# Rows of eight tokens cast by the DMA, masks made by GpSimd, and a new order of sums and scalings in the head of an attention and feed-forward kernel

## The chip, the cores and the metric

The kernel runs on one core of one Trainium2 chip. The metric is the device time of the program in microseconds (us). Each kernel was run beside the kernel before, on the same chip, several rounds in turn. A ratio is the mean time of a kernel's fast runs over that of the kernel before beside it, so it is not quite the ratio of the medians that are quoted. The experiments are compared with each other and with the change by medians, although they did not all run together; the kernel before was at 361.9 to 362.2 us in every group. All runs in this study were in the fast state.

## The reference, cut to what matters

```python
# q, k, v: (8 batches, 8 heads, 576 tokens, 64), f32
rel = pos[:, None] - pos[None, :]
mask_plain = (rel >= 0) & (rel < 32)                            # heads 0 to 3
mask_dil   = (rel >= 0) & (rel < 128) & (rel % 4 == 0)          # heads 4 to 7
attn = softmax(where(mask, q @ k.T / 8, -1e9)) @ v
x = attn.transpose(0, 2, 1, 3).reshape(4608, 512)
out = ((gelu(x @ w_gate) * (x @ w_val)) @ w_out)                # 512 -> 1536 -> 512
```

## The kernel before

One unit of attention is two heads of one batch. The kernel runs the four units of batch 0 alone (the head), then starts the feed-forward on 512 tokens at a time and hides the other units beside it. Dilated heads are split by token modulo 4, so q and k must be transposed with four tokens to a row. These are the loads and helpers that the change touches:

```python
def quads(src, b, h0, lo, hi):           # four tokens to a row: 128 rows + a rest of 16 rows
    return src[b, h0 : h0 + HK, lo:hi, :].rearrange("h (p r) d -> p h (r d)", r=4)

def load_qk_dil(b):                      # GpSimd's queue, cast f32 -> f16 by the DMA
    qd = ldp.tile([P, 2, HK, 4, D], F16, ...); rd = ldp.tile([16, 2, HK, 4, D], F16, ...)
    for t, src in ((0, q), (1, k)):
        nc.gpsimd.dma_start(out=fl(qd[:, t]), in_=quads(src, b, HK, 0, 4 * P))
    for t, src in ((0, q), (1, k)):
        nc.gpsimd.dma_start(out=fl(rd[:, t]), in_=quads(src, b, HK, 4 * P, S))
```

The head itself, in program order (cut):

```python
# plain q, k of batch 0 on the SP and ACT queues (f32); identity and masks from DRAM on GpSimd's
for t, src, eng in ((0, q, nc.sync), (1, k, nc.scalar)):
    eng.dma_start(out=fh(first_d[t]), in_=quads(src, 0, HK, 0, 4 * P))     # dilated, f32
    eng.dma_start(out=fh(first_r[t]), in_=quads(src, 0, HK, 4 * P, S))
v_plain(0, sv0, nc.sync)                                                   # values, f32
...
load_v_dil_rest(0)
load_w(0)                        # first block of gate and value weights
v_cast(0, sv0)                   # GpSimd; waits for the values
copy("pool", tiles["v", 0][1], r4(first_vd))
w1 = load_w(1)
load_w(2)
...
emit_s(0, 4, pe_mask=True); emit_s(1, 0, pe_mask=True)      # scores of units 0 and 1
...                                                         # den(): sums, num(): numerators
num(2, 0); num(3, 2)
gate["dma"] = w1
...                              # batch 1: plain q, k on SP's queue, then
qd1, rd1 = load_qk_dil(1)
load_wo(0)
... cast_six("pool", q61, st1, t, hp)                       # needs batch 1's plain q and k
wo1 = load_wo(1); wo2 = load_wo(2)
```

In the first feed-forward pass (c == 0) TensorE transposes batch 1 between column blocks: dilated after blocks 8 and 11, plain after blocks 9 and 10. The prediction calls each of these places a hook.

The softmax here doesn't subtract the row's maximum and nothing guards it: scores larger than these inputs give would overflow.

Of the kernel before, what the change touches and what calls it, by code (L numbers as in the profile page):

```python
# [9 lines left out]
F16 = mybir.dt.float16  # L10
F32 = mybir.dt.float32
# [7 lines left out]


def _np_masks():
    p = np.arange(128)[:, None]

    def band(n, off=0):
        rel = np.arange(n)[None, :] + off - p
        return (rel >= 0) & (rel < WIN)

    main_p, last_p, tail_p = band(160), band(128), band(64, 64)
    main_d = band(128)

    rel = 48 + np.arange(16)[None, :] - p % 64
    rest_d = [(rel >= 0) & (rel < WIN) & (p // 64 == m) for m in range(2)]
    mp = np.concatenate([main_p, main_p, main_p, last_p, tail_p], axis=1).astype(np.float16)
    md = np.concatenate([main_d, rest_d[0], main_d, rest_d[1]], axis=1).astype(np.float16)
    return mp, md
# [3 lines left out]
def kernel(  # L39
# [19 lines left out]
    R6 = S // 6  # L59
    NCH = NT // CH  # L60
# [10 lines left out]

    mp_np, md_np = _np_masks()
    mp_dram = nc.inline_tensor(mp_np, name="mask_plain")
    md_dram = nc.inline_tensor(md_np, name="mask_dil")
    id_dram = nc.inline_tensor(np.eye(P, dtype=np.float16), name="attn_identity")
    id32_dram = nc.inline_tensor(np.eye(16, dtype=np.float32), name="identity_f32")
# [13 lines left out]
    ident32 = const.tile([16, 16], F32, tag="ident32")  # L90
# [31 lines left out]
    first_d = [x32[t][:, 0 : HK * 4 * D] for t in range(2)]  # L122
    first_r = [x32[2 + t][0:16, 0 : HK * 4 * D] for t in range(2)]
# [21 lines left out]
    def quads(src, b, h0, lo, hi):  # L145

        return src[b, h0 : h0 + HK, lo:hi, :].rearrange("h (p r) d -> p h (r d)", r=4)
# [4 lines left out]
    def fh(t):  # L152
        return t.rearrange("p (h c) -> p h c", h=HK)

    def sixes(src, b):

        return src[b, 0:HK, :, :].rearrange("h (p r) d -> p h (r d)", r=6)

# [44 lines left out]
    def load_qk_dil(b):  # L203
        qd = ldp.tile([P, 2, HK, 4, D], F16, tag="qd", name=f"qd{b}")
        rd = ldp.tile([16, 2, HK, 4, D], F16, tag="rd", name=f"rd{b}")
        for t, src in ((0, q), (1, k)):
            nc.gpsimd.dma_start(out=fl(qd[:, t]), in_=quads(src, b, HK, 0, 4 * P))
        for t, src in ((0, q), (1, k)):
            nc.gpsimd.dma_start(out=fl(rd[:, t]), in_=quads(src, b, HK, 4 * P, S))
        return qd, rd  # L210

# [44 lines left out]
    def copy(eng, dst, src):  # L256
        if eng == "act":
            nc.scalar.copy(dst, src)
        elif eng == "pool":
            nc.gpsimd.tensor_copy(dst, src)  # L260
        else:
            nc.vector.tensor_copy(dst, src)
# [21 lines left out]
    def t_dil(b, hp, qd, q0, k0, engs):  # L284

        qtd_ = tiles["qT", b][1]
        for t, c0 in ((0, q0), (1, k0)):
            for hl in range(2):
                for m in range(2):
                    nc.tensor.transpose(  # L290
                        ps16f[:, c0 + (2 * hl + m) * P : c0 + (2 * hl + m + 1) * P],
                        qd[:, t, 2 * hp + hl, 2 * m : 2 * m + 2, :].rearrange("p r d -> p (r d)"),
                        ident,
                    )
        for t, c0 in ((0, q0), (1, k0)):
            copy(
                engs[t],
                qtd_[:, t, 2 * hp : 2 * hp + 2].rearrange("p h m i -> p (h m) i")[:, :, 0:P],
                ps16f[:, c0 : c0 + 512].rearrange("p (c i) -> p c i", i=P),
            )  # L300

    def t_rest(b, hp, rd, r0):

        qtd_ = tiles["qT", b][1]
        f32 = rd[0].dtype == F32
        pv = (psf if f32 else ps16f)[:, r0 : r0 + P]
        for t in range(2):
            for hl in range(2):
                for m in range(2):
                    c0 = (4 * t + 2 * hl + m) * 16  # L310
                    h0 = (2 * hp + hl) * 4 * D + 2 * m * D
                    nc.tensor.transpose(
                        pv[:, c0 : c0 + 16], rd[t][:, h0 : h0 + P], ident32 if f32 else ident[0:16, 0:16]
                    )
        nc.vector.tensor_copy(
            qtd_[:, :, 2 * hp : 2 * hp + 2].rearrange("p t h m i -> p t (h m) i")[:, :, :, P:NCL],
            pv.rearrange("p (t c i) -> p t c i", t=2, i=16),
        )
# [262 lines left out]
    def warm(n, bank):  # L581
        for _ in range(n):
            nc.tensor.matmul(ps[:, bank, :], ones[:, 0:P], ones, start=True, stop=True)
# [4 lines left out]
    nc.gpsimd.dma_start(ident, id_dram.ap())  # L588
    nc.gpsimd.dma_start(mask_p, mp_dram.ap())
    for t, src, eng in ((0, q, nc.sync), (1, k, nc.scalar)):  # L590
        eng.dma_start(out=fh(first_d[t]), in_=quads(src, 0, HK, 0, 4 * P))
        eng.dma_start(out=fh(first_r[t]), in_=quads(src, 0, HK, 4 * P, S))
    nc.gpsimd.dma_start(ident32, id32_dram.ap())
    nc.gpsimd.dma_start(mask_d, md_dram.ap())
# [5 lines left out]
    qd0 = ldp.tile([P, 2, HK, 4, D], F16, tag="qd", name="qd0")  # L600
# [3 lines left out]

    def r4(t):
        return fh(t).rearrange("p h (r d) -> p h r d", r=4)

    warm(16, 7)
# [6 lines left out]
    nc.vector.tensor_scalar(bias_p, mask_p, 1.0, 60000.0, ALU.subtract, ALU.mult)  # L615
    for hp in range(2):
        t_plain(0, q6, hp, 2 * hp, ("act", "dve"))
    nc.gpsimd.tensor_scalar(bias_d, mask_d, 1.0, 60000.0, ALU.subtract, ALU.mult)
    for hp in range(2):
        copy("pool", qd0[:, 0, 2 * hp : 2 * hp + 2], r4(first_d[0])[:, 2 * hp : 2 * hp + 2])  # L620
    load_v_dil_rest(0)
    load_w(0)
    v_cast(0, sv0)
    copy("pool", tiles["v", 0][1], r4(first_vd))
    w1 = load_w(1)
    load_w(2)
# [8 lines left out]

    emit_s(0, 4, pe_mask=True)
    emit_s(1, 0, pe_mask=True)
    for hp, eng in ((0, "dve"), (1, "act")):
        copy(eng, qd0[:, 1, 2 * hp : 2 * hp + 2], r4(first_d[1])[:, 2 * hp : 2 * hp + 2])
    den(0, 4, wide=True)  # L640
    for hp in range(2):
        t_dil(0, hp, qd0, 4096 + 1024 * hp, 4608 + 1024 * hp, ("act", "dve"))
    for hp in range(2):
        t_rest(0, hp, first_r, P * hp)
    last_keys(0, 0, HK)
    den(1, 4, wide=True)
    emit_s(2, 0, pe_mask=True)
    num(0, 4)
    den(2, 4, wide=True)
    emit_s(3, 0, pe_mask=True)  # L650
    num(1, 4)
    den(3, 4, wide=True)
    num(2, 0)
    num(3, 2)
# [8 lines left out]
    qd1, rd1 = load_qk_dil(1)  # L663
# [28 lines left out]
    for c in range(NCH):  # L692
# [11 lines left out]
        for nb in range(NNB):  # L704
# [19 lines left out]
            if c == 0 and nb in (8, 11):  # L724
                rr = rd1.rearrange("p t h r d -> p t (h r d)")
                hp = nb // 11
                t_dil(1, hp, qd1, 4096 + 512 * hp, 5120 + 512 * hp, ("dve", "dve"))
                t_rest(1, hp, (rr[:, 0], rr[:, 1]), 6144 + P * hp)
# [109 lines left out]
```

## Time and profile before

| | |
|---|---|
| time before, median | 362.28 us (361.33 to 362.37, 3 runs) |
| span of the profiled run | 359.8 us, TensorE (PE) busy 344.5 us |
| first feed-forward matmul | 25.77 us |
| first column pair of the feed-forward done | 30.55 us |
| batch 1's first transpose | 42.64 us |
| first matmul of the output projection | 50.54 us |

In the page and in the timelines, each line gives an engine, a line of the kernel, an operation and what it reads and writes. A bracket at the end says how long the engine had been idle, and what ended that. The granted clock is the share of TensorE's full clock that it was given in a stretch. The prediction below shows the lines of before that carry the reading. Three more of the timeline of before matter later. They are the second place where TensorE meets a load (columns: start us, length us, engine, line, operation):

```profile
42.64 0.61 PE L290 MATMUL ps<-ident,qd 128*128 128x128 f16 x8
43.18 0.38 PE L312 MATMUL ps<-ident,rd 16*128 16x16 f16 x8
43.49 1.04 PE L533 MATMUL ps<-xT,wg 128*128 128x512 f16 x4
```

There is no bracket: batch 1's dilated q and k arrive just in time, and nothing is lost. By the view of the transfers, k's 128 rows land 18.7 us after their issue at 24.05, at 42.75, and its 16 rows 17.6 us after 25.69, at 43.29. "Just in time" is what I failed to see as a danger.

### The profile page before, as it was taken

The numbers are of one execution on the slowest core, as the hardware profiler recorded it, in microseconds if no ns is written. First come the engines' busy times: TensorE is split into PE (matmuls) and PEld (weight loads), VectorE is DVE, ScalarE is ACT, GpSimd is POOL, SyncE is SP. The second block draws the span as 40 slices with busy tenths as digits, with TensorE's granted clock in tenths as the row PEclk, the third lists the DMA queues.
The fourth block names the chain that finished last, engine by engine and source line by source line (L and its number), as shares of the span: only waits on it lengthen the run. The fifth ranks groups of instructions, "written<-read, shape, count | busy, mean of one in ns | idle before, by whom it ended". The sixth has DMA issues, their size and how long they took to land.

```text
span 359.8 us, 5997 instructions
## 1 busy us (share of the span) xinstructions
PE 344.5 (96%) x2358; PEld 166.2 (46%) x2358; DVE 196.0 (54%) x298; ACT 145.9 (41%) x212; POOL 78.2 (22%) x110
## 2 busy tenths in 40 slices
PE   6789999999989999899999999999999999999995
PEld 2554454444544445444444444544454444444442
DVE  3584446744266325765479838893679613403320
ACT  2633355244542345433653356436543123312321
POOL 2580434450531342063003410140000000000000
PEclk9959999999999999999999999999999999999999
DMA  8999999999999897599438952795100020011002
GB/s 208 232 183 215 209 159 195 199 141 239 192 119 228 178 157 144 139 168 153 94 106 186 148 97 88 178 168 68 60 29 0 21 97 2 1 66 52 0 29 87
DMA packets 107291, 45.30 MB, mean 126 GB/s; under 512 B 83040, under 2 KB 102496, under 8 KB 107264
## 3 DMA queue, kind: packets, MB, share of 16 engines
q1 hardware_dynamic: 84272, 31.21, 40.1%
q0 software_dynamic: 21456, 12.01, 25.8%
q10 hardware_dynamic: 1536, 1.70, 2.1%
q8 instruction: 18, 0.29, 0.3%
q14 instruction: 9, 0.07, 0.1%
HBM read 40.13 MB, written 9.44 MB: 138 GB/s over the span
## 4 chain that ended last, share of the span: by engine, by line
PE 88%; DVE 5%; DMA 3%; ACT 1%; issue 1%; ACTq 0%
PE ps L533 47%; PE ps L564 26%; PE ps L442 5%; PE ps L545 4%; DMA xT<-in_k_dram 3%; PE ps L369 2%; PE ps L339 1%; DVE dt L500 1%; DVE rb L507 1%; DVE xT L521 1%; PE ps L355 1%; PE ps L455 1%; PE ps L332 1%; ACT P L371 1%; DVE rc L505 0%
## 5 line engine op out<-in xcount | busy, mean ns | idle before, releaser
L558 DVE SCALAR_TENSOR_TENSOR u_all<-g,ps 128x512 f16<-128x512 f16 x108 | 72.6, 683 | 75.8 <-PE ps L533 65.7
L557 ACT ACTIVATE g<-ps 128x512 f16<-128x512 f32 x108 | 63.6, 597 | 123.6 <-PE ps L533 109.4
L564 PE MATMUL ps<-wo,u_all 128*128 128x512 f16 x432 | 100.9, 380 | 0.4 <-ACT osb L575 0.3
L533 PE MATMUL ps<-xT,wg 128*128 128x512 f16 x392 | 100.6, 379 | 0.2
L533 PE MATMUL ps<-xT,wv 128*128 128x512 f16 x392 | 100.6, 379 | 0.0
L564 PEld LDWEIGHTS <-u_all 128*128 128x128 f16 x432 | 39.2, 98 | 44.6 <-issue 0.5
L533 PEld LDWEIGHTS <-wv 128*128 128x128 f16 x392 | 38.3, 98 | 46.4 <-issue 0.2
L533 PEld LDWEIGHTS <-wg 128*128 128x128 f16 x392 | 37.3, 98 | 44.6 <-issue 2.1
L575 ACT ACTIVATE osb<-ps 128x512 f32<-128x512 f32 x33 | 19.7, 597 | 48.4 <-PE ps L564 48.4
L500 DVE STREAM_TRANSPOSE dt<-ps 128x576 f32<-128x576 f32 x25 | 19.5, 779 | 25.7 <-PE ps L442 25.6
L199 POOL CAST qp<-st 128x2048 f16<-128x2048 f32 x6 | 11.4, 1893 | 99.5 <-DMA st<-in_k_dram 61.3
L507 DVE STREAM_TRANSPOSE rb<-rc 128x576 f32<-128x576 f32 x32 | 24.9, 778 | 1.1
L371 ACT ACTIVATE P<-ps 128x1152 f16<-128x1152 f32 x16 | 18.1, 1129 | 13.1 <-PE ps L369 13.0
L349 ACT ACTIVATE P<-ps 128x960 f16<-128x960 f32 x16 | 15.5, 970 | 9.2 <-PE ps L339 9.1
L521 DVE TENSOR_TENSOR xT<-ps,rb 128x576 f16<-128x576 f32 x16 | 17.8, 1124 | 0.3
L545 PE MATMUL ps<-xT,wg 128*128 128x512 f16 x40 | 16.0, 400 | 1.4 <-DVE xT L521 0.9
L577 DVE TENSOR_SCALAR osb<-ps 128x512 f32<-128x512 f32 x3 | 2.1, 692 | 27.8 <-PE ps L564 27.8
L545 PE MATMUL ps<-xT,wv 128*128 128x512 f16 x40 | 15.9, 398 | 0.0
L442 PE MATMUL ps<-P,ones 128*64 128x192 f16 (+5 forms) x174 | 11.6, 248 | 2.0 <-ACT P L371 1.0
L379 DVE TENSOR_TENSOR P<-P,mask_p 128x1344 f16<-128x1344 f16 x10 | 9.1, 917 | 6.8 <-ACT P L350 6.8
L379 DVE TENSOR_TENSOR P<-P,mask_d 128x1152 f16<-128x1152 f16 x8 | 6.1, 757 | 11.1 <-ACT P L371 11.1
L470 DVE STREAM_TRANSPOSE dt<-ps 64x576 f32<-64x576 f32 x14 | 10.9, 781 | 0.4
(83 smaller groups left out, 268.4 us busy)
## 6 DMA issues: line engine op xcount, KB each, us to landing
out_dram<-osb SPq DMA_DIRECT2D x36, 256.0 KB, 2.0
sv<-in_v_dram SPq DMA_DIRECT2D x40, 128.0 KB, 3.5
st<-in_q_dram SPq DMA_DIRECT2D x24, 128.0 KB, 3.2
st<-in_k_dram SPq DMA_DIRECT2D x24, 128.0 KB, 2.9
qd<-in_q_dram POOLq DMA_DIRECT2D x7, 256.0 KB, 5.0
qd<-in_k_dram POOLq DMA_DIRECT2D x7, 256.0 KB, 6.7
vd<-in_v_dram POOLq DMA_DIRECT2D x7, 256.0 KB, 7.1
wg<-in_moe_w_gate_dram POOLq DMA_DIRECT2D x3, 512.0 KB, 7.7
```

The source lines that it names most:

```text
L349: nc.scalar.activation(pt[:, :, 0:PB], sb[:, 0, :, 0:PB], AF.Exp, bias=0.0, scale=scale)
L371: nc.scalar.activation(pt, ps[:, b0 : b0 + 4, 0:DW], AF.Exp, bias=0.0, scale=scale)
L442: nc.tensor.matmul(o, lhs, rhs, start=st, stop=True, skip_group_check=True)
L500: nc.vector.transpose(dst, den)
L507: nc.vector.transpose(rb.rearrange("p (b c) -> p b c", c=32), bass.AP(tensor=rc.tensor, offset=rc.offset, ap=[rc.ap[0], [1, 18], [0, 32]]),)
L521: nc.vector.tensor_tensor(dst.rearrange("p (i m s) -> p i m s", m=2, s=2), num, rb.rearrange("p (s m i) -> p i m s", s=2, m=2), ALU.mult,)
L533: nc.tensor.matmul(ps[:, b0 + gi, :], w[:, kc, ns], xT[kc][:, tok], start=(kc == 0), stop=(kc == NKC - 1))
L545: nc.tensor.matmul(ps[:, pairs[nb] + gi, :], w[:, kc, ns], xT[kc][:, tok], start=(kc == 0), stop=(kc == NKC - 1),)
L557: nc.scalar.activation(g, ps[:, b0, :], AF.Gelu)
L558: nc.vector.scalar_tensor_tensor(u_all[:, nb, :], g, USCALE, ps[:, b0 + 1, :], ALU.mult, ALU.mult)
L564: nc.tensor.matmul(ps[:, bank, :], u_all[:, fc, tb * P : (tb + 1) * P], wo_t[fc // 4][:, fc % 4, :], start=(fc == 0), stop=(fc == NNB - 1),)
L575: nc.scalar.activation(osb, ps[:, bank, :], AF.Copy, bias=0.0, scale=1.0 / USCALE)
```

## The change

Its intent: fewer bytes and casts in the head, and less for VectorE (DVE) to do there. Batches 0 and 1 load dilated q and k in 72 rows of eight tokens, cast by the DMA. Identity and masks are made by GpSimd (POOL). The sums of batch 0 get their own PSUM banks, and two units are scaled by GpSimd. Core of the diff, cuts marked:

```diff
+def load_eights(b):
+    q8 = ldp.tile([R8, 2, HK, 8, D], F16, tag="qd", name=f"qd{b}")        # R8 = 72
+    for t, src in ((0, q), (1, k)):
+        nc.gpsimd.dma_start(out=q8[:, t].rearrange("p h r d -> p h (r d)"), in_=eights(src, b, HK, H))
...
-nc.gpsimd.dma_start(ident, id_dram.ap()); nc.gpsimd.dma_start(mask_p, mp_dram.ap())   # and mask_d
-    eng.dma_start(out=fh(first_d[t]), ...); eng.dma_start(out=fh(first_r[t]), ...)
+mask_plain()                     # GpSimd: fill, six affine selects
+qd0 = load_eights(0)
+mask_dil()
...
 load_v_dil_rest(0)
-load_w(0)
 v_cast(0, sv0)
+load_w(0)
...
+def num_split(n, b0):
+    emit_pv(n, b0, ("num",))
+    rb = tiles.pop(("rb", n))
+    nc.scalar.copy(first_n[n], psf[:, b0 * 512 : b0 * 512 + S])
+    nc.gpsimd.tensor_tensor(xT[n][:, 0:S], first_n[n], rb, ALU.mult)
...
+t_dil(0, 0, qd0, 4, ("dve", "dve")); t_dil(0, 1, qd0, 6, ("act", "act"))
+... copy("pool", tiles["v", 0][1], r4(first_vd)); w1 = load_w(1)
+den(0, 0, wide=True); den(1, -2, wide=True)
+emit_s(2, 4, ...); emit_s(3, 0, ...)
+num_split(0, 4); den(2, 4, ...); num_split(1, 0); ...; den(3, 4, ...); norm_x(2, 2); num(3, 0)
+load_w(2)
...
-qd1, rd1 = load_qk_dil(1)
+qd1 = load_eights(1)
```

More of the change, by code (lines that the diff above doesn't have):

```diff
@@ L18 @@
 USCALE = 32.0
-def _np_masks():
-    p = np.arange(128)[:, None]
-    def band(n, off=0):
-        rel = np.arange(n)[None, :] + off - p
-        return (rel >= 0) & (rel < WIN)
-    main_p, last_p, tail_p = band(160), band(128), band(64, 64)
-    main_d = band(128)
-    rel = 48 + np.arange(16)[None, :] - p % 64
-    rest_d = [(rel >= 0) & (rel < WIN) & (p // 64 == m) for m in range(2)]
-    mp = np.concatenate([main_p, main_p, main_p, last_p, tail_p], axis=1).astype(np.float16)
-    md = np.concatenate([main_d, rest_d[0], main_d, rest_d[1]], axis=1).astype(np.float16)
-    return mp, md
 @with_exitstack
@@ L59 @@
     R6 = S // 6
+    R8 = S // 8
     NCH = NT // CH
@@ L70 @@
     ctx.enter_context(tc.manual_schedule())
-    mp_np, md_np = _np_masks()
-    mp_dram = nc.inline_tensor(mp_np, name="mask_plain")
-    md_dram = nc.inline_tensor(md_np, name="mask_dil")
-    id_dram = nc.inline_tensor(np.eye(P, dtype=np.float16), name="attn_identity")
-    id32_dram = nc.inline_tensor(np.eye(16, dtype=np.float32), name="identity_f32")
     const = ctx.enter_context(tc.tile_pool(name="const", bufs=1))
@@ L89 @@
     ident = const.tile([P, P], F16, tag="ident")
-    ident32 = const.tile([16, 16], F32, tag="ident32")
     mask_p = const.tile([P, PH], F16, tag="mask_p")
@@ L121, with band, mask_plain, mask_dil @@
     first_p = u32[0:R6, :].rearrange("p (t h c) -> p t h c", t=2, h=HK)
-    first_d = [x32[t][:, 0 : HK * 4 * D] for t in range(2)]
-    first_r = [x32[2 + t][0:16, 0 : HK * 4 * D] for t in range(2)]
+    first_n = [x32[g][:, 0:S] for g in range(2)]
+    nc.gpsimd.memset(ident, 1.0)
+    for sign in (1, -1):
+        nc.gpsimd.affine_select(
+            out=ident, in_=ident, pattern=[[sign, P]], compare_op=ALU.is_ge, fill=0.0, base=0, channel_multiplier=-sign
+        )
+    def band(t, step, off):
+        for sign, base in ((1, off), (-1, WIN - 1 - off)):
+            nc.gpsimd.affine_select(
+                out=t,
+                in_=t,
+                pattern=[[sign * step, t.shape[1]], [sign, t.shape[2]]],
+                compare_op=ALU.is_ge,
+                fill=0.0,
+                base=base,
+                channel_multiplier=-sign,
+            )
+    def mask_plain():
+        nc.gpsimd.memset(mask_p, 1.0)
+        band(mask_p[:, 0:PB].rearrange("p (r c) -> p r c", c=PW), 0, 0)
+        band(mask_p[:, PB : PB + P].rearrange("p (r c) -> p r c", r=1), 0, 0)
+        band(mask_p[:, PB + P : PH].rearrange("p (r c) -> p r c", r=1), 0, 64)
+        nc.vector.tensor_scalar(bias_p, mask_p, 1.0, 60000.0, ALU.subtract, ALU.mult)
+    def mask_dil():
+        nc.gpsimd.memset(mask_d, 1.0)
+        by_class = mask_d.rearrange("p (m i) -> p m i", m=2)
+        band(by_class[:, :, 0:P], 0, 0)
+        band(by_class[:, :, P:NCL], 64, 48)
     def load_w(i):
@@ L157, in sixes, with eights @@
         return src[b, 0:HK, :, :].rearrange("h (p r) d -> p h (r d)", r=6)
+    def eights(src, b, h0, h1):
+        return src[b, h0:h1, :, :].rearrange("h (p r) d -> p h (r d)", r=8)
     def rows(src, b, kb):
@@ L210, in load_qk_dil @@
         return qd, rd
+    def load_eights(b):
+        q8 = ldp.tile([R8, 2, HK, 8, D], F16, tag="qd", name=f"qd{b}")
+        for t, src in ((0, q), (1, k)):
+            nc.gpsimd.dma_start(out=q8[:, t].rearrange("p h r d -> p h (r d)"), in_=eights(src, b, HK, H))
+        return q8
     def load_v_dil(b):
@@ L282, in t_plain, with t_dil @@
             )
-    def t_dil(b, hp, qd, q0, k0, engs):
+    def t_dil(b, hp, q8, b0, engs):
         qtd_ = tiles["qT", b][1]
-        for t, c0 in ((0, q0), (1, k0)):
+        for t in range(2):
             for hl in range(2):
-                for m in range(2):
+                for r in range(4):
+                    c0 = ((hl * 2 + r % 2) * 2 + r // 2) * R8
                     nc.tensor.transpose(
-                        ps16f[:, c0 + (2 * hl + m) * P : c0 + (2 * hl + m + 1) * P],
-                        qd[:, t, 2 * hp + hl, 2 * m : 2 * m + 2, :].rearrange("p r d -> p (r d)"),
-                        ident,
+                        ps16[:, b0 + t, c0 : c0 + R8],
+                        q8[:, t, 2 * hp + hl, 2 * r : 2 * r + 2, :].rearrange("p r d -> p (r d)"),
+                        ident[0:R8, 0:R8],
                     )
-        for t, c0 in ((0, q0), (1, k0)):
             copy(
                 engs[t],
-                qtd_[:, t, 2 * hp : 2 * hp + 2].rearrange("p h m i -> p (h m) i")[:, :, 0:P],
-                ps16f[:, c0 : c0 + 512].rearrange("p (c i) -> p c i", i=P),
-            )
-    def t_rest(b, hp, rd, r0):
-        qtd_ = tiles["qT", b][1]
-        f32 = rd[0].dtype == F32
-        pv = (psf if f32 else ps16f)[:, r0 : r0 + P]
-        for t in range(2):
-            for hl in range(2):
-                for m in range(2):
-                    c0 = (4 * t + 2 * hl + m) * 16
-                    h0 = (2 * hp + hl) * 4 * D + 2 * m * D
-                    nc.tensor.transpose(
-                        pv[:, c0 : c0 + 16], rd[t][:, h0 : h0 + P], ident32 if f32 else ident[0:16, 0:16]
-                    )
-        nc.vector.tensor_copy(
-            qtd_[:, :, 2 * hp : 2 * hp + 2].rearrange("p t h m i -> p t (h m) i")[:, :, :, P:NCL],
-            pv.rearrange("p (t c i) -> p t c i", t=2, i=16),
-        )
+                qtd_[:, t, 2 * hp : 2 * hp + 2].rearrange("p h m (i u) -> p (h m) i u", u=2),
+                ps16[:, b0 + t, 0:S].rearrange("p (c u i) -> p c i u", c=4, u=2),
+            )
     def emit_s(n, b0, pe_mask=False):
@@ L587 @@
         eng.dma_start(out=first_p[:, t], in_=sixes(src, 0))
-    nc.gpsimd.dma_start(ident, id_dram.ap())
-    nc.gpsimd.dma_start(mask_p, mp_dram.ap())
-    for t, src, eng in ((0, q, nc.sync), (1, k, nc.scalar)):
-        eng.dma_start(out=fh(first_d[t]), in_=quads(src, 0, HK, 0, 4 * P))
-        eng.dma_start(out=fh(first_r[t]), in_=quads(src, 0, HK, 4 * P, S))
-    nc.gpsimd.dma_start(ident32, id32_dram.ap())
-    nc.gpsimd.dma_start(mask_d, md_dram.ap())
+    mask_plain()
+    qd0 = load_eights(0)
+    mask_dil()
     sv0 = new_v(0)
@@ L599 @@
     q6 = ldp.tile([R6, 2, 6, HK, D], F16, tag="qp", name="qp0")
-    qd0 = ldp.tile([P, 2, HK, 4, D], F16, tag="qd", name="qd0")
     new_qt(0)
-    def r4(t):
-        return fh(t).rearrange("p h (r d) -> p h r d", r=4)
-    warm(16, 7)
+    warm(22, 7)
     for vp_, _, vt_, _ in vset:
@@ L614, with r4 @@
             cast_six(("dve", "act")[t], q6, first_p, t, hp)
-    nc.vector.tensor_scalar(bias_p, mask_p, 1.0, 60000.0, ALU.subtract, ALU.mult)
     for hp in range(2):
         t_plain(0, q6, hp, 2 * hp, ("act", "dve"))
-    nc.gpsimd.tensor_scalar(bias_d, mask_d, 1.0, 60000.0, ALU.subtract, ALU.mult)
-    for hp in range(2):
-        copy("pool", qd0[:, 0, 2 * hp : 2 * hp + 2], r4(first_d[0])[:, 2 * hp : 2 * hp + 2])
+    nc.vector.tensor_scalar(bias_d, mask_d, 1.0, 60000.0, ALU.subtract, ALU.mult)
     load_v_dil_rest(0)
+    v_cast(0, sv0)
     load_w(0)
-    v_cast(0, sv0)
-    copy("pool", tiles["v", 0][1], r4(first_vd))
-    w1 = load_w(1)
-    load_w(2)
+    def r4(t):
+        return fh(t).rearrange("p h (r d) -> p h r d", r=4)
     def den(n, b0, wide=False):
@@ L634, in num @@
         norm_x(n, b0)
+    def num_split(n, b0):
[3 more added lines that the diff above has]
+        nc.gpsimd.tensor_tensor(xT[n][:, 0:S], first_n[n], rb, ALU.mult)
     emit_s(0, 4, pe_mask=True)
     emit_s(1, 0, pe_mask=True)
-    for hp, eng in ((0, "dve"), (1, "act")):
-        copy(eng, qd0[:, 1, 2 * hp : 2 * hp + 2], r4(first_d[1])[:, 2 * hp : 2 * hp + 2])
-    den(0, 4, wide=True)
-    for hp in range(2):
-        t_dil(0, hp, qd0, 4096 + 1024 * hp, 4608 + 1024 * hp, ("act", "dve"))
-    for hp in range(2):
-        t_rest(0, hp, first_r, P * hp)
-    last_keys(0, 0, HK)
-    den(1, 4, wide=True)
-    emit_s(2, 0, pe_mask=True)
-    num(0, 4)
+    t_dil(0, 0, qd0, 4, ("dve", "dve"))
+    t_dil(0, 1, qd0, 6, ("act", "act"))
+    last_keys(0, 0, 2)
+    last_keys(0, 2, HK, nc.gpsimd)
+    copy("pool", tiles["v", 0][1], r4(first_vd))
+    w1 = load_w(1)
+    den(0, 0, wide=True)
+    den(1, -2, wide=True)
+    emit_s(2, 4, pe_mask=True)
+    emit_s(3, 0, pe_mask=True)
+    num_split(0, 4)
     den(2, 4, wide=True)
-    emit_s(3, 0, pe_mask=True)
-    num(1, 4)
+    num_split(1, 0)
+    emit_pv(2, 2, ("num",))
     den(3, 4, wide=True)
-    num(2, 0)
-    num(3, 2)
+    norm_x(2, 2)
+    num(3, 0)
+    load_w(2)
     gate["dma"] = w1
@@ L724 @@
             if c == 0 and nb in (8, 11):
-                rr = rd1.rearrange("p t h r d -> p t (h r d)")
-                hp = nb // 11
-                t_dil(1, hp, qd1, 4096 + 512 * hp, 5120 + 512 * hp, ("dve", "dve"))
-                t_rest(1, hp, (rr[:, 0], rr[:, 1]), 6144 + P * hp)
+                t_dil(1, nb // 11, qd1, 6 - 2 * (nb // 11), ("dve", "dve"))
             if nb == NNB - 1 and c > 0 and s_list:
```

## The prediction

> **What bounds the kernel now.** I read first the page's slices of the span, then the chain of waits in order of time, then the timeline of the first 31 us engine by engine, the DMA issues of the first 45 us, and the table of 5 us windows.
>
> The slices tell which part of the kernel can move at all:
>
> ```profile
> PE   6789999999989999899999999999999999999995
> PEclk9959999999999999999999999999999999999999
> ```
>
> One slice is 9 us. TensorE (PE) is full from the fourth slice on; only the first three are thin, and the granted clock falls only in the third (18 to 27 us). In the table of windows PE is busy 5.00 of every 5 us from 25 to 55 us. After the head the kernel is a stream of matmuls which the change touches only where batch 1 is transposed. So the question is: when do the first feed-forward matmuls (L545) begin, and at what clock?
>
> The chain of waits (start us, length us, what) answers the first half:
>
> ```profile
> 1.19 12.33 DMA xT<-in_k_dram
> 14.07 0.78 DVE dt L500
> 15.17 0.78 DVE rb L507
> 15.95 0.64 DVE qTd L262 x2
> ...
> 24.10 1.73 PE ps L442 x24
> 25.83 4.88 PE ps L545 x16
> 30.72 12.09 PE ps L533 x56
> ```
>
> For 12.3 us the chain is one transfer, the dilated k of batch 0 in f32, landing at 13.52. Then follow 12.3 us of short steps to 25.8. The first 16 feed-forward matmuls take 4.9 us instead of some 3.45 (16 at the 0.216 us between starts that the timeline shows at full clock), because they begin at half clock: the windows give a granted clock of 0.50 in 20 to 25 us and 0.65 in 25 to 30 us.
>
> The timeline (start us, us, engine, line, operation) shows VectorE (DVE) is the busiest on that path, and GpSimd (POOL) spends its time on issuing:
>
> ```profile
> 13.54 0.60 DVE L262 CAST qd<-xT 128x512 f16<-128x512 f32 x1 [2.18 <-DMA xT<-in_k_dram]
> 19.20 0.78 DVE L507 STREAM_TRANSPOSE rb<-rc 128x576 f32<-128x576 f32 x1
> 20.04 0.76 DVE L518 TENSOR_TENSOR xT<-ps,rb 128x576 f16<-128x576 f32 x1
> 10.37 1.19 POOL L618 TENSOR_SCALAR bias_d<-mask_d 128x288 f16<-128x288 f16 x1 [6.82 <-DMA mask_d<-mask_dil]
> 16.64 0.78 POOL L128 DMA_DIRECT2D wv<-in_moe_w_val_dram  x1
> ```
>
> A second limit lies just under the first. The view of the tile wv gives 8.8 us as its shortest issue-to-landing time. Its first issue at 16.64 plus 8.8 is 25.4, and PE takes it at 25.8. So DMA must come earlier too if the start is to move.
>
> [...] masks issued on the software queue at 1.9 and 3.0 us landed 7.8 and 7.3 us later, while 1.15 MB of plain q and k was running. [...] the clock falls after the transposes of 13.9 to 17.5 us, and matmul spacing returns from 0.43 to 0.22 us at 28.3, 2.5 us after the dense stream begins.
>
> **The change part by part.**
>
> *Loads.* The masks (168, 72, 32 and 1 KB) are no longer loaded. Dilated q and k of batch 0 leave the hardware queues and are cast by the DMA. Cost: over the first 45 us, plain transfers on the SP queue use 28.4% of 45 us for 3.02 MB, 4.2 us per MB; the software queue uses 66.4% for 4.67 MB written, 6.4 us per MB. Before, 1.18 MB plain is 5.0 us and masks some 1.7 us; after, 0.59 MB cast is 3.8 us. Saving: 2.9 us of DMA time. But GpSimd issues this load only after building mask_p. Its casts run at 1.0 to 1.3 ns per column, its two-step bias at 4.1; I take 1.75 plus 0.15 us per instruction as an estimate for a select. Identity: 256 columns, two instructions, 0.75 us. Plain mask: 1344 columns, six instructions, 3.25 us. Fills: 0.8 us. Begun at 0.6, this ends at 5.4; two issues of 0.8 end at 7.0. Before, the same load was issued at 1.2. And values, formerly behind it, now compete. From 2.0 us: plain q and k 4.8 us, values (1.15 MB) 4.9, casting load 3.8, sum 13.5, so all lands by about 15.5. [...] k at T = 14.8. The same sum for before (2.0 + 4.8 + 5.0 + 1.7 = 13.5) hits the observed 13.52.
>
> *Chain from T.* PE transposes: 32 of 72 columns instead of 16 of 128 plus 16 small ones. At the 64 ns of the present plain ones (18 in 1.16 us), 24 wait for k: 1.5 us. In program order, the sums of units 0 and 1 now follow them: 0.5 us each, first at T+2.0. DVE's reciprocal chain is 0.78 + 0.27 + 0.78, with gaps 1.9 us; unit 1's sums are read by T+4.7, freeing banks 0 and 1. Scores of unit 3: bias 1.07 and products 0.61 at half clock, T+6.4. Then PE alone: numerator 0 (0.8), sums 2 (0.7), numerators 1 and 2 (0.8, 1.0), sums 3 (0.7), numerator 3 (1.0): T+11.4. Meanwhile ScalarE (ACT) ends unit 3's exponential at T+7.5, copies numerator 0 by T+8.15 (0.64, as 576 columns cost at 45.69 us)[...]. DVE ends its last scaling at T+14.5, before half-clock PE needs it. So the step from landing to feed-forward shrinks from 12.25 to 11.4: the two DVE scalings (1.5 us) and a cast (0.6) leave, but sums now wait for transposes. Start: 14.8 + 11.4 = 26.2 against 25.8, **0.4 us later**.
>
> *Weights.* First weights are issued after the value cast, which waits for values: about 14 to 15.5 instead of 15.9. At 2.8 us per weight transfer (landings 8.8 us after 16.64 and 6.7 after 15.87 are 2.9 apart), both land by 23 and do not bound. The third weight block goes out about 26 instead of 21.9, yet is needed only at eight column blocks, about 41.
>
> *Batch 1.* Half as many issues; PE 16 transposes of 55 to 64 ns (0.9 to 1.0 us) per hook against 0.61 + 0.38 at present: nothing. DVE copies 0.7 twice instead of 0.37 twice plus 0.21, some 0.45 us more per hook; the second can hold bank 5 before the scores of unit 4, for at most 0.3 us. No change to the other 300 us.
>
> Sum: +0.4 from the head, +0.2 from batch 1, about -0.9 because the DMA saving may bring landing or clock forward more than this queue sum allows. I choose 362.0.
>
> **Rivals.** First, *earlier landing*: if the engines share well and GpSimd needs only 1 ns per column, T is 12.5 to 13 and the start 24 to 24.5: 360 to 360.7. For it: 2.9 us of DMA time vanish, and rate falls to 118 GB/s around 12 us before, perhaps due to small pieces. Against it: values now come first. Second, *GpSimd becomes the bound*: at the 4.1 ns of its present bias, masks take about 7 us and the issue ends near 11[...]. T is 16 to 17.5, the time 363.5 to 365. [...] Fourth, *DMA hides all*: if weights still land at 25.5, the time stays at 362.3.
>
> **Range and chances.** The landing carries the error: T between 12.5 and 17.2 moves the time one for one around the base, giving 359.6 to 364.8 eight times in ten. Two per cent is 7.2 us. Faster by that would put the start at 18.5, before the chain can end: 0.02. Slower needs T above 21: 0.04. Within: 0.94.
>
> **What would show it.** The landing of the casting k load near 14.8 (shown by the first batch-0 dilated copy), issued near 6 to 7; GpSimd selects near 1.75 ns per column; [...] unit 3's scores waiting for DVE's read of unit 1's sums; L545 starting near 26 at half clock; PE full from there. It is wrong if selects cost several times more, if the load crawls beside the values, or if the clock stays full.

## The result, and the profile after

The time is 365.23 us (364.15 to 365.75, 4 runs) against 361.93 us (361.33 to 362.37, 4 runs) for the kernel before. The ratio is 1.0088, with a 95% interval of 1.006 to 1.0117. The change costs 0.9%: within 2%, as forecast, but above the upper end of 364.8 us.

The same landmarks in the two profiled runs show where the time went:

| us from the start | before | after | after minus before |
|---|---|---|---|
| first feed-forward matmul | 25.77 | 24.61 | -1.16 |
| first column pair done | 30.55 | 29.30 | -1.25 |
| block 9 begins, after the first dilated transposes | 43.49 | 45.27 | +1.78 |
| first plain transpose, after block 9 | 45.23 | 48.30 | +3.07 |
| output projection begins | 50.54 | 53.29 | +2.75 |
| end of span | 359.8 | 362.4 | +2.6 |

So the head became 1.25 us **faster**, and then some 4.3 us were lost between 41 and 48 us. The timeline of TensorE after the change, at the place shown for before:

```profile
42.38 0.43 PE L311 MATMUL ps<-ident,qd 72*128 72x72 f16 x8 [0.83 <-DMA qd<-in_q_dram]
44.81 0.66 PE L311 MATMUL ps<-ident,qd 72*128 72x72 f16 x8 [1.99 <-DMA qd<-in_k_dram]
45.27 1.90 PE L535 MATMUL ps<-xT,wg 128*128 128x512 f16 x4
46.97 1.49 PE L535 MATMUL ps<-xT,wv 128*128 128x512 f16 x4
```

TensorE waits 0.83 us for batch 1's q and 1.99 us for its k. The eight matmuls after that take 3.03 us from start to the next transpose; before, at a granted clock of 1.00, they took 1.74. The table of windows says why. Its columns are the stretch and its length; then busy us (and instructions) of PE, weight load, DVE, ACT and POOL; then granted clock, DMA share and GB/s. First before:

```profile
15.50:16.50 1.00, 0.39 (x7) 0.29 (x5) 1.00 (x3) 0.41 (x1) 1.00 (x2) 1.00 1.35 223
16.50:17.50 1.00, 0.66 (x10) 0.63 (x12) 0.29 (x2) 0.00 (x0) 0.92 (x2) 1.00 1.68 215
41.00:45.00 4.00, 4.00 (x32) 2.12 (x31) 2.17 (x5) 1.03 (x2) 2.99 (x4) 1.00 0.91 144
45.00:48.00 3.00, 3.00 (x35) 1.92 (x34) 1.60 (x3) 1.47 (x4) 2.80 (x5) 1.00 0.67 104
```

and after:

```profile
15.50:16.50 1.00, 0.94 (x26) 0.88 (x28) 0.40 (x1) 0.20 (x1) 1.00 (x3) 1.00 0.31 29
16.50:17.50 1.00, 1.00 (x15) 0.65 (x15) 0.96 (x3) 0.97 (x2) 1.00 (x2) 0.84 0.06 16
41.00:45.00 4.00, 1.18 (x15) 0.56 (x14) 1.45 (x2) 0.33 (x1) 1.46 (x2) 0.93 1.13 164
45.00:48.00 3.00, 3.00 (x15) 1.31 (x13) 0.76 (x1) 0.60 (x1) 3.00 (x5) 0.52 0.22 36
```

Two things stand out. From 41 to 45 us PE works 1.18 of 4 us instead of all 4, and its clock then falls to 0.52. And from 15.5 to 17.5 us the DMA, which moved 215 to 223 GB/s before, moves 16 to 29 GB/s: it has almost nothing to do. The chain of waits after the change (start us, length us, what) suggests a link between the two:

```profile
3.52 11.14 DMA sv<-in_v_dram
14.82 1.04 POOL vp L197
16.20 0.71 POOL wg L137
...
25.86 0.80 POOL wg L137
26.67 0.75 POOL wv L138
27.41 0.72 POOL qd L229
28.14 16.62 DMA qd<-in_k_dram
44.81 0.66 PE ps L311 x8
```

The head's path to the feed-forward no longer appears in it. The chain is now GpSimd's order of issue: it waits for the values, casts them, then issues the first weights, and so on to the last transfer. One link of it is loose: in the part cut out, GpSimd stands for 2.66 us from 20.45, and the timeline further below shows that it waits there for ScalarE's copy of a numerator. So late first weights do not by themselves make the later issues late; if they matter, it is through the transfers that pile up. This gives three candidate causes.

- **A**: the first weights wait behind the value cast, the DMA stands still for 2.5 us, and everything behind is late.
- **B**: the third weights and batch 1's load are issued late, behind GpSimd's scalings.
- **C**: the load of 72 rows is slow in itself.

### The profile page after: what moved, and what is told of

Its sections match the earlier page's. It is cut to its first block, busy times and chain, and to the rows that moved or that the text cites. A ratio compares the mean times of both kernels' runs of the same rounds, so it can differ in the third digit from the quotient of the medians.

```text
span 362.4 us, 6012 instructions
## 1 busy us (share of the span) xinstructions
PE 345.8 (95%) x2364; PEld 165.7 (46%) x2364; DVE 195.1 (54%) x292; ACT 146.6 (40%) x213; POOL 81.6 (23%) x121
## 4 chain that ended last, share of the span: by engine, by line
PE 82%; DMA 8%; DVE 4%; POOL 3%; issue 1%; ACT 1%; SPq 1%; POOLq 0%; ACTq 0%; DVEq 0%
PE ps L535 44%; PE ps L566 26%; DMA qd<-in_k_dram 5%; PE ps L444 4%; DMA sv<-in_v_dram 3%; PE ps L547 3%; PE ps L371 1%; PE ps L341 1%; DVE xT L523 1%; PE ps L457 1%; DVE dt L502 1%; DVE rb L509 1%; PE ps L357 1%; PE ps L334 1%; POOL wv L138 1%
## 5 line engine op out<-in xcount | busy, mean ns | idle before, releaser
L566 PE MATMUL ps<-wo,u_all 128*128 128x512 f16 x432 | 100.9, 380 | 0.4 <-ACT osb L577 0.3
L566 PEld LDWEIGHTS <-u_all 128*128 128x128 f16 x432 | 39.2, 98 | 44.5 <-issue 0.5
L213 POOL CAST qp<-st 128x2048 f16<-128x2048 f32 x6 | 11.4, 1894 | 104.7 <-DMA st<-in_k_dram 73.6
L351 ACT ACTIVATE P<-ps 128x960 f16<-128x960 f32 x16 | 15.5, 970 | 8.8 <-PE ps L341 8.7
L197 POOL CAST vp<-sv 128x1024 f16<-128x1024 f32 x8 | 8.5, 1064 | 15.9 <-DMA sv<-in_v_dram 15.9
```

What stands on the lines that cost most here:

```text
L351: nc.scalar.activation(pt[:, :, 0:PB], sb[:, 0, :, 0:PB], AF.Exp, bias=0.0, scale=scale)
L566: nc.tensor.matmul(ps[:, bank, :], u_all[:, fc, tb * P : (tb + 1) * P], wo_t[fc // 4][:, fc % 4, :], start=(fc == 0), stop=(fc == NNB - 1),)
```

## The experiments

Fourteen kernels were run. Except where the text says otherwise, each edits the changed kernel; every one gave correct results. The kernel before ran beside them at 362.1 to 362.2 us. A caution for the profiles: between 20 and 25 us the granted clock was anything from 0.50 to 1.00 in these single runs (0.60 after, 0.50 in the first run below, 1.00 in the third), and the start of the feed-forward moved by up to 1.5 us with it. The timed medians carry the verdicts. The profiles carry the waits and landings.

### First weights ahead of the value cast

```diff
 load_v_dil_rest(0)
+load_w(0)
 v_cast(0, sv0)
-load_w(0)
```

> The change with one line moved: the first weight block is issued ahead of the cast of batch 0's values, as before the change. Theory A (DMA starvation: the first weights wait behind the value cast, the DMA stands still from 15.5 to 18 us and everything behind it lands 2 to 2.5 us later): no gap in the DMA rate at 15.5 to 18 us, the casting k load of batch 1 lands at 42 to 43 us instead of 44.8, TensorE's wait at the first transpose of batch 1 falls from 2.8 us to under 1 us, the clock stays full there, time 361 to 362.5 us. Theory B (third weights issued late, behind GpSimd's scalings): the wait stays, time 365. Theory C (the 72-row load itself is slow): the wait shrinks little, time 364 to 365.

Measured: 362.22 us, ratio 1.0009 (0.9981 to 1.0037). The time is as A expected, 3.0 us below the change. The landing is not. The timeline of this kernel:

```profile
44.35 0.43 PE L311 MATMUL ps<-ident,qd 72*128 72x72 f16 x8 [1.04 <-DMA qd<-in_k_dram]
44.62 1.03 PE L535 MATMUL ps<-xT,wg 128*128 128x512 f16 x4
```

k lands at 44.35, half a microsecond earlier, not two. The gap at 15.5 us is gone, but the DMA now runs dry around 21 us and again from 27 to 30 us, because the second and third weights still wait for GpSimd. In this profile TensorE also came later (feed-forward from 26.11), waited 1.04 us, and kept its clock: four matmuls take 1.03 us. Counted from the start of the feed-forward, k does come two microseconds earlier, 18.2 us after it instead of 20.2. So the order of issue is worth time, but this run alone does not show that it is the landing of k.

### Third weights ahead of GpSimd's scalings

```diff
 w1 = load_w(1)
+load_w(2)
 ...
-load_w(2)
```

> The change with the third weight block issued right after the second, ahead of GpSimd's scalings. Theory A (starvation at 15.5 to 18 us): the DMA queue was never empty between 18.5 and 41 us, so nothing moves: 365 +- 0.5 us. Theory B (the late issue of the third block delays batch 1): the casting k load of batch 1 lands 2 us or more earlier, time 362 to 363. Theory C: 365.

Measured: 364.34 us, ratio 1.0066 (1.004 to 1.0092). That is a little under the expected 365 +- 0.5, and nowhere near B's 362 to 363. The interval overlaps that of the change (1.006 to 1.0117), so the 0.9 us are not clear of noise. In the timeline of this kernel k is no earlier and the clock drops again (0.62 from 45 to 48 us):

```profile
45.05 0.43 PE L311 MATMUL ps<-ident,qd 72*128 72x72 f16 x8 [1.84 <-DMA qd<-in_k_dram]
45.32 1.53 PE L535 MATMUL ps<-xT,wg 128*128 128x512 f16 x4
```

B falls. While A's gap and the 72 rows stay, issuing the third weights earlier gains little.

### Batch 1 loaded in the old form

```diff
-qd1 = load_eights(1)
+qd1, rd1 = load_qk_dil(1)       # and the old transposes for batch 1
```

> The change, but batch 1's dilated q and k loaded as before the change (128 rows of four tokens plus 16 rows), with the old transposes. Theory C (72 rows use fewer DMA engines, so this load is slow): lands 1.5 to 2.5 us earlier than 44.8 us, time 362.5 to 363.5. Theory A and B: within 0.5 us of 365.

Measured: 361.97 us, ratio 0.9996 (0.9971 to 1.0021): 3.3 us recovered, more than expected. The timeline of this kernel shows k in time, with the DMA gap at 15.5 us still there:

```profile
41.23 0.40 PE L328 MATMUL ps<-ident,qd 128*128 128x128 f16 x4
42.44 0.40 PE L328 MATMUL ps<-ident,qd 128*128 128x128 f16 x4 [0.82 <-DMA qd<-in_k_dram]
```

C stands: the same bytes in 128 and 16 rows land at 42.4 instead of 44.8 us.

### Batch 1's transposes moved to later blocks

```diff
-if c == 0 and nb in (9, 10): t_plain(1, q61, nb - 9, ...)
-if c == 0 and nb in (8, 11): t_dil(1, nb // 11, qd1, ...)
+if c == 0 and nb in (10, 11):   # dilated 0, plain 0 after block 10; plain 1, dilated 1 after 11
```

> The change with batch 1's transposes moved from after blocks 8 to 11 to after blocks 10 and 11; loads untouched. If TensorE's wait for the load is what costs (2.8 us of idling and about 1.3 us of halved clock after it), the wait disappears although the load still lands at 44 to 45 us, up to 0.7 us comes back as waits for copies: 361.5 to 362.5 us. If the loss lies elsewhere (later stages, output): 364 to 365.

Measured: 365.04 us, ratio 1.0073 (1.0048 to 1.0098). A clear miss: the wait moved and did not vanish. In the timeline of this kernel the output projection (L566) now waits twice for its weights:

```profile
52.27 0.38 PE L566 MATMUL ps<-wo,u_all 128*128 128x512 f16 x1 [2.05 <-DMA wo<-in_moe_w_out_dram]
```

Those weights are issued by GpSimd after it has cast batch 1's plain q and k, which land late as well. So it is not one load that is late but the whole stream of transfers, and TensorE meets it at whichever tile it needs next.

### The old kernel with rows of eight in batch 1 alone

```diff
# on the kernel BEFORE
-qd1, rd1 = load_qk_dil(1)
+qd1 = load_eights(1)            # and the new transposes for batch 1
```

> The kernel before with one part of the change alone: batch 1's dilated q and k in 72 rows of eight tokens. Theory C (either form): k lands 2 us or more later than the 42.7 us of before, TensorE waits at the transposes near 43 us, time 363.5 to 365. If the rows of eight are harmful only together with the later issue and the DMA gap of the change: 362 to 362.8.

Measured: 364.75 us, ratio 1.0064 (1.0039 to 1.0089). This one part costs 2.6 us without any of the others. TensorE waits only 0.66 us at the transposes. Its long wait is again the output weights. From the timelines of this kernel, PE first, then GpSimd's issue:

```profile
56.36 0.81 PE L593 MATMUL ps<-wo,u_all 128*128 128x512 f16 x3 [2.46 <-DMA wo<-in_moe_w_out_dram]
46.63 1.51 POOL L134 DMA_DIRECT2D wo<-in_moe_w_out_dram  x2
```

In the kernel before, GpSimd issued these at 44.33 us. The plain q and k of batch 1 are on another queue, but they land later beside the 72-row load (they were issued 0.5 us later, and the casts that wait for them start 1.9 and 2.3 us later), so GpSimd's casts and then its next issues come 2.3 us later. One more thing differs: the first output weights were issued at 25.07 instead of 28.35. In the kernel before, that issue waits 2.15 us for an older weight transfer, landed at 28.06, whose completion semaphore it uses again. They stand behind k on the same queue.

### The same load cut into 64 and 8 rows

```diff
 def load_eights(b):
-        nc.gpsimd.dma_start(out=q8[:, t]..., in_=eights(...))
+        for lo, hi in ((0, 64), (64, R8)) if b else ((0, R8),):
+            nc.gpsimd.dma_start(out=q8[lo:hi, t]..., in_=eights(...)[lo:hi])
```

> The change with batch 1's casting load of 72 rows cut into two transfers, 64 rows and 8 rows; same bytes, same 2 KB pieces, same place in the queue. Theory C1 (72 rows are spread over only some of the 16 DMA engines, so the loaded engines run on after the others): k lands at 42 to 43.3 us instead of 44.8, the DMA rate falls off sharply instead of over 3 us, time 361.5 to 363. Theory C2 (it is the 2 KB pieces or rows of eight tokens that are slow): no change, 364.5 to 365.5.

Measured: 362.97 us, ratio 1.0024 (1.0001 to 1.0047): 2.3 us recovered with the same bytes and pieces. In the timeline of this kernel k lands a microsecond earlier:

```profile
43.78 0.42 PE L314 MATMUL ps<-ident,qd 72*128 72x72 f16 x8 [2.03 <-DMA qd<-in_k_dram]
```

So in the profiles about 1.0 us of this is landing, and the clock stays full (1.00 from 45 to 48 us), which is the 1.3 us lost by eight matmuls after the change. The clock's part cannot be credited to the cut with certainty: here it stays full after 2.65 us without a full-size matmul (41.38 to 44.03), and with the third weights early it fell after 2.53 (42.79 to 45.32).

### 68 and 4 rows, 36 and 36 rows

The edit is that of the last run with 68, then 36, in place of 64.

> The change with batch 1's casting loads cut into 68 and 4 rows: same bytes, same pieces, same number of transfers as the cut into 64 and 8. [...] this must be much worse than the change although the cut is almost the same: [...] k lands 5 us or more after 44.8, time 369 to 376. [...] if cutting alone helps, like 64 and 8: 362.5 to 363.5.

> The change with batch 1's casting loads cut into 36 and 36 rows. [...] it is as good as 64 and 8: 362.5 to 363.5. [...] as bad as the change or worse: 365 to 366.

The two ranges for 36 and 36 are two cases: 362.5 to 363.5 if the cut spreads the load as well as 64 and 8, 365 to 366 if it does not.

Measured: 367.43 us, ratio 1.0149 (1.0122 to 1.0176), for 68 and 4; 363.96 us, ratio 1.005 (1.0028 to 1.0073), for 36 and 36. In the timeline of 68 and 4, TensorE takes q and k together, 1.9 us later than it takes k in the change:

```profile
46.74 1.12 PE L314 MATMUL ps<-ident,qd 72*128 72x72 f16 x16 [5.59 <-DMA qd<-in_q_dram]
```

Moving four rows from one transfer to the other costs 4.5 us. Bytes and number of transfers are the same, so what costs is how the rows are divided. My expected size for 68 (369 to 376) was an estimate that no trace had shown, and too large; the sum below shows why. 36 and 36 came out half a microsecond above what I had expected, 1.3 us below the change, and its interval overlaps that of the change. In its profile TensorE takes k at 44.94, no earlier than in the change; but GpSimd, later in this profile, issued it at 30.27 instead of 28.14.

The DMA's rate from 37 to 57 us, in slices of half a microsecond, shows the spread itself. The four lines are, in this order, the change (72), then 64 and 8, 68 and 4, and 36 and 36:

```profile
GB/s 226 189 213 193 197 205 218 203 169 174 195 203 184 156 121 113 82 47 18 0 35 35 53 168 217 201 199 203 203 203 207 201 130 174 196 204 175 187 240 304
```
```profile
GB/s 256 252 229 239 228 208 231 218 249 225 206 213 199 188 111 41 4 0 0 0 43 43 186 197 203 207 193 176 205 205 193 160 157 206 183 181 182 221 255 273
```
```profile
GB/s 210 224 199 174 215 176 173 161 164 150 179 168 145 145 129 81 104 90 98 98 102 98 35 0 0 0 37 59 182 195 193 205 195 182 207 205 203 164 159 192
```
```profile
GB/s 257 230 231 201 227 233 239 218 231 219 237 223 213 207 207 180 43 39 20 8 0 0 43 51 160 197 188 137 201 188 209 201 233 184 108 179 191 188 186 208
```

Read each line until it falls to nothing. With 64 and 8 or 36 and 36 the rate falls from 200 to under 50 GB/s within about 1 us. With 72 it hangs at 121, 113 and 82 on the way down, and the mean busy share of the 16 DMA engines in these three slices is 0.7, 0.6 and 0.5. With 68 it stays near 100 for three microseconds, at a share of 0.5 to 0.7 in most of them: about half of the engines still work.

No view names the engine of a packet. But the packed trace itself keeps the times of the sixteen counts with which each transfer reports its landing; read as one count for each engine, they show the dealing. In the change, batch 0's q has four counts from 12.13 to 12.19 us and twelve from 12.69 on; its k has eight up to 14.57 and eight from 15.14 on. That fits twelve engines with rows and four without, then eight with twelve rows and eight with six. With both batches cut (below), all sixteen counts of each of batch 0's 64-row transfers come within 0.6 us. With 68 and 4, the 68 rows of batch 1's q have twelve counts by 42.29 and the other four from 46.06 to 46.40, and those of k have eight by 43.95 and eight from 46.16. In batch 1 of the change the groups are less clean (k: seven by 42.95, nine from 43.60).

My estimate from these counts: 72 rows on twelve engines are six each, and q and k, leaving out different fours, put 12 rows on eight engines and six on the others. 68 rows on the four late engines are 17 each, and q and k together load eight so. 64 rows on sixteen are four each. For 64 and 8 I take all 144 rows as evenly spread, nine to an engine; that the small transfers even out was not shown for itself. A row is 4 KB as written, and at 206 GB/s (the rate of the best version below, 25 to 30 us) over 16 engines one engine writes some 12.9 GB/s. So 12 instead of nine rows are 0.95 us (measured against 64 and 8: k 1.03 us later), and 17 instead of 12 are 1.6 us (measured: 1.9, from 44.81 to 46.74). The measurements agree with the estimate. How many engines another number of rows would get was not shown.

### 1 KB pieces

```diff
-nc.gpsimd.dma_start(out=q8[:, t]..., in_=eights(src, b, HK, H))           # batch 1
+for x in range(2): nc.gpsimd.dma_start(out=q8[:, t, x], in_=eights(...)[:, :, 256 * x : 256 * x + 256])
```

> The change with each of batch 1's two casting loads cut by tokens: 72 rows of the first four tokens, then 72 rows of the last four, so the pieces are 1 KB instead of 2 KB; four transfers, as in the run cut by rows (362.97, k landed at 43.8). If the size of a piece is what still separates that run from the old 128-row form (361.97, k at 42.4): k lands at 42 to 43, time 361.5 to 362.5. If only the spread of rows over engines counts, and four transfers of 72 rows spread as well as 64 + 8: like that run, 362.5 to 363.5. If 72 rows stay badly spread: 364.5 to 365.5.

Measured: 362.98 us, ratio 1.0018 (0.9996 to 1.0039): the same as 64 and 8. TensorE takes k at 44.94 in this profile, outside the landing that I had expected, after an issue at 30.17. Smaller pieces add nothing. My estimate: four transfers of 72 rows, on twelve engines each as in the counts above, load all engines evenly if each leaves out another four. The times of this run and of 36 and 36 rows fit an even load; their dealing itself was not shown.

### Both batches cut, and the order of issue by itself

Two runs tell how the causes add. The first cuts the loads of both batches into 64 and 8. The second takes the old load for batch 1 and issues the first weights ahead of the value cast.

> The same cut in both batches. Theory C1: batch 0's k lands 0.5 to 1.2 us earlier than 15.5 us, the feed-forward starts up to 1 us earlier unless the first weights (issued after the value cast) hold it; with batch 1 as in the other run, 361 to 363. Theory C2: 365.

> The change with batch 1 loaded as before the change AND the first weights issued ahead of the value cast. If the idle DMA at 15.5 to 18 us (theory A) costs time on its own, this is 1 us or more below the run with the old batch-1 load alone (361.97): 360.3 to 361. If the order of issue matters only while batch 1's load is late, 361.7 to 362.3.

Measured: 363.93 us, ratio 1.0047 (1.0026 to 1.0068), and 359.78 us, ratio 0.9935 (0.9916 to 0.9954). With both cut, batch 0's k lands 0.6 us earlier (14.9) and the first column pair is done at 28.2, but nothing of it survives: TensorE now waits 0.8 us for the first weights and 2.9 us at the transposes, and the clock halves again (0.52 from 45 to 48 us). That misses the expected 361 to 363, and is 1.0 us above the run with batch 1 alone cut, though the two intervals overlap. A faster head only runs sooner into a stream of transfers that is as late as before.

The second shows A's own worth: 2.2 us below the run that differs from it only in the order of issue (361.97). In that run TensorE had waited 0.9 us for the first weights, 0.8 for k and 0.6 for output weights. With the new order all three waits are absent from the list of its waits. That the order of issue costs is shown by this. That it costs through the empty DMA is argued only: in the 359.78 us kernel the DMA runs dry as well, later (0 to 47 GB/s from 26.5 to 28.5 us).

### What the head's parts are worth

Two more runs edit the 359.78 us kernel. One scales batch 0's units with VectorE again (`num` for both `num_split`), the other loads identity and masks by DMA as before.

> The 359.78 kernel with the two units of batch 0 scaled by VectorE again instead of ScalarE's copy and GpSimd's multiply; sums still in own banks. If that part of the change carries the gain of the head (2.4 us under the kernel before), the time rises by 1 to 2 us: 360.8 to 361.8. If VectorE has room there: 359.5 to 360.3.

> The 359.78 kernel with identity and masks loaded by DMA as before the change instead of made by GpSimd. The load of q8 and k8 is then issued about 1 us earlier or at the same time, but 0.27 MB of mask (some 1.3 us of DMA time at the rates measured) competes: batch 0's k lands 0 to 1 us later, time 359.5 to 361. If the masks carry the gain: over 361.

Measured: 361.66 us, ratio 0.9982 (0.9961 to 1.0003), and 363.96 us, ratio 1.0054 (1.0032 to 1.0075). The scaling by ScalarE and GpSimd is worth about 1.9 us, as expected, and that although GpSimd, free of it, issues the third weights at 21.37 instead of 26.07. From the list of TensorE's waits (waits in us in total, times, longest) in the run with VectorE:

```profile
PE ps L480 <- DVE xT L556: 1.1, 1, 1.1
```

The masks are a surprise, and the run does not isolate them. From its list of waits, and its GpSimd timeline:

```profile
PE ps L396 <- POOL kTr L240: 3.2, 1, 3.2
19.66 1.04 POOL L186 CAST vp<-sv 128x1024 f16<-128x1024 f32 x1 [10.16 <-DMA sv<-in_v_dram]
```

Without masks to make, GpSimd issued the first weights at 5.8 us instead of 9.6. It seems that they crowded out the values: GpSimd then waited ten microseconds for them ahead of the value cast, and a small copy that TensorE needs waited behind it. So making the masks also set the time at which the first weights were issued. What the masks cost or save by themselves stays open.

### The best version

```diff
# the 359.78 us kernel, with
 w1 = load_w(1)
+load_w(2)                       # ahead of GpSimd's scalings
+ # batch 0's load cut into 64 and 8 rows
```

> Candidate for the best version: old batch-1 load, first weights ahead of the value cast (359.78 so far), plus third weights ahead of GpSimd's scalings, plus batch 0's casting load cut into 64 and 8 rows. In the 359.78 run the DMA stands still from 26 to 28.5 us, but TensorE waits for nothing after 28 us, so filling that gap should bring nothing; the cut should bring the feed-forward forward by 0.5 to 1 us: 358.7 to 359.5. If the gap did cost: below 358.7.

Measured: 359.20 us (358.29 to 359.96, 6 runs), ratio 0.9916 (0.9895 to 0.9937). It beats the kernel before by 0.84% and the change by about 1.7%. The two lines of its timeline that matter are batch 0's k and the start of the feed-forward:

```profile
14.91 0.94 PE L314 MATMUL ps<-ident,qd 72*128 72x72 f16 x24 [1.04 <-DMA qd<-in_k_dram]
23.94 0.38 PE L586 MATMUL ps<-xT,wg 128*128 128x512 f16 x1
```

Both are 0.9 us earlier than in the 359.78 us kernel (15.77 and 24.82), and TensorE waits for no transfer after that. The intervals of the two ratios overlap, so the last step is likely, not certain, and the run does not separate its two edits.

## Why the prediction was wrong

- **What bounds the kernel: half right.** The head did get shorter, in the way the chain of waits said. But I read the chain's entry from 30.72 us on as "a stream of matmuls" and looked for waits only in the head. The transposes at 42.64 us had no slack at all.
- **GpSimd's masks: right.** The eight selects of identity and plain mask took 3.0 us together, against 4.0 in the sum, my estimate between the casts of before (0.41 us for 256 columns, 1.04 for 1024) and its two-step bias (1.19 for 288); the six over 1344 columns took 2.38 us, 1.8 ns a column with all overheads; the loads of batch 0 were issued at 4.7 and 5.6 us. From the timeline after, the plain mask's selects, then the scalings:

```profile
2.42 2.38 POOL L111 TENSOR_SCALAR_AFFINE_SELECT mask_p<-mask_p 128x480 f16<-128x480 f16 x6
23.15 2.76 POOL L631 TENSOR_TENSOR xT<-xT,rb 128x576 f16<-128x576 f32 x2 [2.70 <-ACT xT L630]
```

- **The head as a whole: luck in part.** The sum had +0.4 us for it and -0.9 us without a working, together -0.5; the first column pair came 1.25 us earlier. Two errors worked against each other, as the next two points show: k came 0.8 us later than predicted, and the chain from there took 2.35 us less.
- **Landing of k: slightly off.** TensorE took it at 15.56, estimated at 14.8, although the issue was earlier than predicted. By the runs on batch 1, the uneven deal of 72 rows is in this too: cut into 64 and 8 it was taken at 14.9.
- **Chain from landing to feed-forward: mis-sized.** Predicted 11.4 us, measured 9.05 (15.56 to 24.61). Scores of unit 3 did wait for VectorE's read of unit 1's sums (0.77 us), and the scalings took 1.38 us each. But the numerators and sums took 3.3 us in place of 5.0, and the granted clock was 0.50 from 23 to 24 us and 1.00 from 24 us on, so the first column pair took 4.7 us with waits for scaled units, not for a slow clock.
- **Weights: failed.** "About 14 to 15.5 ... and do not bound." They were issued at 16.15, after the values landed at 14.8, and meanwhile the DMA ran empty (16 to 29 GB/s). TensorE did not wait for them in this profile; the cost came later, through the transfers behind them. I had checked when the weights were needed, not what the engines would do until their issue. By the runs with the old batch-1 load, this costs 2.2 us. The third weights, issued at 25.86 against "about 26", did no harm clear of noise.
- **Batch 1: the step that failed most.** "Half as many issues; ... nothing." I counted instructions and copies and did not ask how 72 rows load. It costs 2.6 us on the kernel before and 3.3 us in the change: k landed at 44.8 us and TensorE waited 2.8 us for q and k at a place that it had passed without a wait.
- **The rivals.** None put a loss at the transposes of batch 1. There the granted clock was 0.52 from 45 to 48 us, after TensorE had waited 2.8 us, and eight matmuls took 1.3 us more. That the wait lowers the clock was not shown: with 64 and 8 rows TensorE waited 2.03 us for k and the clock stayed at 1.00.
- **Slips in the working.** One for one, landings of 12.5 to 17.2 give 359.7 to 364.4 us, not 359.6 to 364.8, and 2% slower needs a landing near 22, not 21. The 1.15 MB of plain q and k are the 1.18 MB of the dilated ones (576 KB twice). The full clock at 28.3 us is 2.5 us after the first feed-forward matmul, but TensorE had been without a gap since 24.10, 4.2 us before, so the reading as 2.5 us does not hold.

The account in medians: with both faults undone the change takes 359.8 us, 2.4 us below the kernel before. With only the first weights moved, 362.2. With only the old batch-1 load, 362.0. With neither, 365.2. Mending either fault recovers some 3 us, mending both 5.4.

**Still open**: 64 and 8 rows (362.97) remain 1.0 us above the old form (361.97). The intervals of their ratios overlap, and neither piece size nor number of transfers was shown to explain it. The masks' own worth is open too, and so is what made the granted clock differ between runs, in the head and after batch 1's transposes.

## What to carry to other kernels

When a change rewrites a load, ask how its rows divide over the DMA engines, and look at how its rate falls at the end. Here twice 72 rows left, by my estimate from the counts, eight engines with half the rows of the others: the rate hung at 121 to 82 GB/s for 1.5 us, and in the kernel before with rows of eight in batch 1 alone, casts that wait for another queue's transfers started 1.9 and 2.3 us later. 64 and 8 rows recovered 2.3 us. When an engine both computes and issues transfers, a wait put ahead of an issue can empty the DMA, here to 16 to 29 GB/s from 15.5 to 17.5 us; check the order of issue against the arrival of what it waits for. And a load that arrives just in time can be on the critical path of the next change, even if no profile line of today shows a wait: k landed at 42.75 without a wait before, and TensorE waited 2.8 us for q and k after.
